# The first k load: from ScalarE's DMA queue to SyncE's, between q and v

## The chip, the cores and the metric

The kernel runs on one core of a Trainium2 chip. The metric is the device time of one launch in microseconds (us). The time before is the median of 3 runs; the profile is of one further execution of the same program.

## The reference

Inputs are q, k and v of shape [8, 8, 576, 64] (batch, heads, positions, head width) and the weights of a mixture of experts, all fp32. What is computed, cut to what matters:

```python
scores = q @ k^T / 8
# heads 0..3: 0 <= i - j < 32
# heads 4..7: 0 <= i - j < 128 and (i - j) % 4 == 0
attn = softmax(where(mask, scores, -1e9))
x = (attn @ v) laid out as [8 * 576, 512]         # 4608 rows, heads side by side

logits = x @ phi                                  # phi [512, 32]: 8 experts, 4 slots each
d = softmax of logits over the 4608 rows          # dispatch
slot_input = d^T @ x                              # [32, 512]
slot_out = relu(slot_input @ w1[e]) @ w2[e]       # w1 [8, 512, 1024], w2 [8, 1024, 512]
out = (softmax of logits over the 32 slots) @ slot_out
```

## The kernel before

**Units and batches.** A unit is a pair of heads of one batch: 4 units to a batch, 32 in all, two pairs of plain windows and two of dilated ones. A loop over u (line 665) runs the stages of neighbouring units one behind the other: scores of the next unit, `values` of this one, the exponentials and masks, the transposes of q and k three units ahead, and the transposes of x of the unit before. Per batch there are also the logits, row weights and slot sums of the batch before, and the selection of v's rows for the next batch. The experts come after the last batch, then the output rows in nine tiles of 512.

**Loads.** Nearly everything is loaded by GpSimd (POOL), whose DMAs turn fp32 into fp16 on the way. For each batch `load_batch` (L179) issues six to seven loads into a buffer, the batch's home. There are eight homes of 16 KB per partition. When a batch is done with, its home takes expert weights (`load_w1`, `load_w2` and others, L266 to L311); a weight load thus waits until the batch that had its home is finished with. The order of POOL's instructions is that of the program (`manual_schedule`, L639).

**The first loads.** Three transfers don't go through POOL, since they are to come before all others: q and k of the first two heads of batch 0 (288 KB each) and v of the first four heads (512 KB). They are loaded as fp32 into `stage`, which takes home 7's place until batch 7 needs it. DVE then casts q and k (L209, one instruction each) while it sets the two heads side by side, PE transposes them (L342), ACT copies the transposes out of PSUM (L343), and the first scores follow. v is cast on ACT (`cast_first_v`, L231), and `select_v` (L238) picks its rows. In the kernel before, q's load is issued by SyncE (SP) and k's by ScalarE (ACT), both on line 74, and v's by SP after q's on line 78. SP issues nothing else until the output (L846, L852).

**Order of the rest.** Two stretches, the head (L644 to L664) and the tail (L702 to L865), have their order on PE, DVE and ACT written out by hand. Before, between and outside them a planner orders the instructions of each engine by its own reckoning. Before the head DVE fills constants (L84 to L126), makes the identity that the transposes need (L148, L149), and does the two casts.

The parts of the kernel that the change touches, with the line numbers of the profile:

Of the kernel before, what the change touches and what calls it, by code (L numbers as in the profile page):

```python
# [46 lines left out]
def kernel(  # L47
# [10 lines left out]
    nc = tc.nc  # L58
# [10 lines left out]
    fixed = keep.tile([128, 128 + QW + 64], FP16, name="fixed")  # L69
    ident, mask = fixed[:, 0:128], fixed[:, 128:]  # L70
    first = {}
    for n, (nm, ten, by) in enumerate((("qp", q, nc.sync), ("kp", k, nc.scalar))):
        first[nm] = stage[0:NP, 768 * n : 768 * n + 768].rearrange("p (g x) -> p g x", g=2)
        by.dma_start(
            out=first[nm],
            in_=ten[0, 0:2].rearrange("h s d -> (h s) d").rearrange("(g p r) d -> p g (r d)", g=2, r=RP),
        )
# [821 lines left out]
```

## Time and profile before

| | |
|---|---|
| median of 3 runs | 180.26 us (180.25 to 180.77) |
| the profiled execution | 180.76 us |
| its span, first to last instruction | 178.5 us |
| mean granted TensorE clock | 0.925 |
| busy: PE, DVE, ACT, POOL | 141.9, 127.6, 117.2, 46.6 us |
| DMA | 41.28 MB in 28,726 packets; HBM read 61.93 MB, written 9.44 MB |

The span counts from the first instruction of any engine to the last; the 2.26 us between it and the execution's time lie around it. Times in the trace are microseconds from the span's start. A line of the timeline gives the start, the duration, the engine (ACTq, SPq and POOL's DMA_DIRECT2D lines are issues of DMAs, not the transfers), the line of the kernel, the operation, output and input, and in brackets how long the engine had been idle and what it waited for. A line of the waits gives who waited for whom: total us, how often, the longest. The DMA queues are named by number: q0 is POOL's, q1 SP's and q10 ACT's. A queue's row gives packets, MB, and the time that its packets took as a share of what 16 engines have.

### The profile page before, as it was taken

The numbers are of one execution on the slowest core, as the hardware profiler recorded it, in microseconds if no ns is written. First come the engines' busy times: TensorE is split into PE (matmuls) and PEld (weight loads), VectorE is DVE, ScalarE is ACT, GpSimd is POOL, SyncE is SP. The second block draws the span as 40 slices with busy tenths as digits, with TensorE's granted clock in tenths as the row PEclk, the third lists the DMA queues.
The fourth block names the chain that finished last, engine by engine and source line by source line (L and its number), as shares of the span: only waits on it lengthen the run. The fifth ranks groups of instructions, "written<-read, shape, count | busy, mean of one in ns | idle before, by whom it ended". The sixth has DMA issues, their size and how long they took to land.

```text
span 178.5 us, 5128 instructions
## 1 busy us (share of the span) xinstructions
PE 141.9 (80%) x2137; PEld 96.7 (54%) x2137; DVE 127.6 (72%) x360; ACT 117.2 (66%) x217; POOL 46.6 (26%) x74
## 2 busy tenths in 40 slices
PE   6697889889999898989989989999689963897000
PEld 2365666575776676667577667666484421542000
DVE  7968998979889789789798988858821110699300
ACT  2568579878897897897988889777321300699100
POOL 7766444444443544000020050042111100000000
PEclk9988699999999999999999999999996996699855
DMA  5999999999999999999999999999999999999996
GB/s 157 240 199 203 201 199 204 200 205 203 203 200 205 201 204 201 224 218 209 224 213 215 224 207 220 220 206 226 215 206 224 208 196 195 242 385 424 431 420 270
DMA packets 28726, 41.28 MB, mean 231 GB/s; under 512 B 1440, under 2 KB 26016, under 8 KB 26144
## 3 DMA queue, kind: packets, MB, share of 16 engines
q0 software_dynamic: 23712, 30.41, 97.1%
q1 hardware_dynamic: 4784, 10.26, 15.0%
q10 hardware_dynamic: 208, 0.29, 0.6%
q8 instruction: 16, 0.26, 0.5%
q14 instruction: 6, 0.05, 0.1%
HBM read 61.93 MB, written 9.44 MB: 400 GB/s over the span
## 4 chain that ended last, share of the span: by engine, by line
PE 38%; DMA 19%; ACT 16%; DVE 14%; issue 4%; POOL 3%; DVEq 0%; ACTq 0%; POOLq 0%
DMA home<-in_moe_w_dram 14%; PE o L486 9%; PE rgx L506 6%; ACT qT L343 5%; PE l L524 5%; DMA home<-in_q_dram 5%; ACT pr L407 4%; PE sel L256 4%; DVE x L491 4%; ACT ot L834 4%; DVE P L433 3%; PE s L381 3%; PE sel L245 3%; PE f L830 3%; PE u L587 2%
## 5 line engine op out<-in xcount | busy, mean ns | idle before, releaser
L491 DVE TENSOR_TENSOR x<-o,rc 128x640 f16<-128x640 f32 x32 | 26.3, 822 | 0.4
L414 ACT ACTIVATE pd<-s 128x640 f16<-128x640 f32 x32 | 21.9, 713 | 2.2 <-PE s L390 2.2
L407 ACT ACTIVATE pr<-s 128x960 f16<-128x960 f32 (+1 forms) x32 | 22.8, 764 | 0.0
L836 DVE TENSOR_SCALAR ot<-f,rrow 128x256 f32<-128x256 f32 (+1 forms) x24 | 13.0, 612 | 6.9 <-PE f L830 6.9
L486 PE MATMUL o<-vd,P 128*128 128x65 f16 x256 | 14.6, 198 | 3.6 <-DVE x L491 3.0
L486 PEld LDWEIGHTS <-P 128*128 128x128 f16 x288 | 12.3, 100 | 7.5 <-DVE x L491 4.1
L512 ACT COPY xT<-rgx 128x512 f16<-128x512 f16 x16 | 9.4, 589 | 10.6 <-PE rgx L506 10.6
L423 DVE TENSOR_TENSOR Pp<-pr,fixed 128x1280 f16<-128x1280 f16 (+1 forms) x32 | 15.6, 501 | 0.1
L486 PE MATMUL o<-vp,Pp 128*128 128x65 f16 x288 | 15.4, 197 | 0.0
L506 PE MATMUL rgx<-fixed,x 128*128 128x128 f16 x155 | 14.0, 222 | 1.7 <-ACT qT L358 0.8
L272 POOL DMA_DIRECT2D home<-in_moe_w_dram x5 | 3.2, 635 | 45.6 <-PE rgq L353 44.1
L343 ACT COPY qT<-rgq 128x576 f16<-128x576 f16 x16 | 10.2, 639 | 6.8 <-PE rgq L342 6.1
L215 POOL DMA_DIRECT2D home<-in_q_dram x15 | 10.0, 668 | 16.2 <-DMA home<-in_v_dram 11.8
L433 DVE TENSOR_TENSOR P<-pd,fixed 128x1024 f16<-128x1024 f16 x16 | 10.9, 679 | 4.7 <-ACT pd L414 4.7
L189 POOL DMA_DIRECT2D home<-in_v_dram x17 | 11.9, 702 | 8.5 <-DMA home<-in_k_dram 4.0
L486 PEld LDWEIGHTS <-Pp 128*128 128x128 f16 x288 | 11.9, 100 | 3.8 <-issue 2.1
L506 PEld LDWEIGHTS <-x 128*128 128x128 f16 x160 | 10.2, 98 | 6.7 <-issue 4.4
L834 ACT ACTIVATE ot<-f,rrow 128x256 f32<-128x256 f32 (+1 forms) x24 | 12.2, 600 | 2.2 <-PE f L830 1.4
L358 DVE COPY kTd<-rgk 128x576 f16<-128x576 f16 x16 | 12.4, 775 | 1.3 <-PE rgk L353 1.3
L830 PE MATMUL f<-so,ET 128*128 128x256 f16 (+1 forms) x48 | 11.4, 361 | 2.2 <-ACT ot L834 1.0
L343 ACT COPY kTp<-rgk 128x576 f16<-128x576 f16 x16 | 10.3, 644 | 2.0 <-PE rgk L342 2.0
L358 ACT COPY qT<-rgq 128x576 f16<-128x576 f16 x16 | 10.3, 641 | 2.0 <-PE rgq L353 1.4
(133 smaller groups left out, 319.0 us busy)
## 6 DMA issues: line engine op xcount, KB each, us to landing
home<-in_moe_w_dram POOLq DMA_DIRECT2D x5, 2048.0 KB, 35.5
home<-in_q_dram POOLq DMA_DIRECT2D x15, 288.0 KB, 10.2
home<-in_k_dram POOLq DMA_DIRECT2D x15, 288.0 KB, 11.0
home<-in_moe_w_dram POOLq DMA_DIRECT2D x4, 1024.0 KB, 28.0
out_dram<-ot SPq DMA_DIRECT2D x4, 1024.0 KB, 9.4
home<-in_v_dram POOLq DMA_DIRECT2D x6, 512.0 KB, 12.7
out_dram<-ot SPq DMA_DIRECT2D x4, 512.0 KB, 3.8
out_dram<-ot SPq DMA_DIRECT2D x1, 2048.0 KB, 7.7
```

The source lines that it names most:

```text
L343: nc.scalar.copy(out=dst[:, 0:S].rearrange("c (p r) -> c p r", r=RP), in_=rg.rearrange("c r p -> c p r"),)
L358: (nc.scalar.copy if nm == "q" else nc.vector.tensor_copy)(out=dst[:, 0:S].rearrange("c (g p a) -> c g p a", g=4, a=3), in_=rg.rearrange(" ...
L407: nc.scalar.activation(out=(pr[:, :, 0 : 3 * QW], pr[:, :, 3 * QW :])[part], in_=st[:, :, 0 : (480, 224)[part]], func=AF.Exp, scale=SCALE,)
L414: nc.scalar.activation(out=pr[:, part].rearrange("p c e t -> p e c t"), in_=st[:, :, 0 : 2 * DW].rearrange("p e (c t) -> p e c t", c=2), f ...
L423: nc.vector.tensor_tensor(out=Pp[:, :, b0 : b0 + nb, 0:w], in0=pr[:, :, b0 * QW : b0 * QW + nb * w].rearrange("p h (t c) -> p h t c", c=w) ...
L433: nc.vector.tensor_tensor(out=P1.rearrange("p a c t -> p (a c) t"), in0=pr[:, :, :, 0:128].rearrange("p a c t -> p (a c) t"), in1=mask[:, ...
L486: nc.tensor.matmul(ot[:, h, blk], lhs, rhs, start=(n == 0), stop=(n == len(mms) - 1), skip_group_check=True)
L491: nc.vector.tensor_tensor(out=xs[b][:, :, 2 * D * hp : 2 * D * hp + 2 * D].rearrange("p t (h d) -> p h t d", h=2), in0=ot[:, :, :, 0:D], i ...
L506: nc.tensor.transpose(rg[:, 128 * blk : 128 * blk + 128], x[:, blk, hl : hl + 128], ident)
L830: nc.tensor.matmul(fp, ET[:, c0 : c0 + 127 * nj + 1 : nj], so[:, d0:d1], start=True, stop=True)
L834: nc.scalar.activation(out=ot[:, j], in_=fp, func=AF.Copy, scale=scale)
L836: nc.vector.tensor_scalar(out=ot[:, j], in0=fp, scalar1=scale, scalar2=None, op0=ALU.mult)
```

## The change

k's load of the first two heads is issued by SyncE in place of ScalarE. In the program it stands after q's load and before v's, all three on SyncE's queue. ScalarE then issues no DMA in the whole kernel. The bytes, the shapes, the destinations and all other instructions in the program are the same.

```diff
@@ -69,9 +69,9 @@
     fixed = keep.tile([128, 128 + QW + 64], FP16, name="fixed")
     ident, mask = fixed[:, 0:128], fixed[:, 128:]
     first = {}
-    for n, (nm, ten, by) in enumerate((("qp", q, nc.sync), ("kp", k, nc.scalar))):
+    for n, (nm, ten) in enumerate((("qp", q), ("kp", k))):
         first[nm] = stage[0:NP, 768 * n : 768 * n + 768].rearrange("p (g x) -> p g x", g=2)
-        by.dma_start(
+        nc.sync.dma_start(
             out=first[nm],
             in_=ten[0, 0:2].rearrange("h s d -> (h s) d").rearrange("(g p r) d -> p g (r d)", g=2, r=RP),
         )
```

## The prediction

> **What bounds the kernel now.** I read the page's slices first, then the chain that ended last, the waits, POOL's timeline, the end, and last the start, where the change is.
>
> The slices of the page:
>
> ```profile
> PE   6697889889999898989989989999689963897000
> ...
> DMA  5999999999999999999999999999999999999996
> GB/s 157 240 199 203 201 199 204 200 205 203 203 200 205 201 204 201 224 218 209 224 213 215 224 207 220 220 206 226 215 206 224 208 196 195 242 385 424 431 420 270
> ```
>
> One slice is 4.46 us. The 16 DMA engines are full from the second slice to the last; only the first has room, half of it. Some 200 to 220 GB/s written is full: POOL's loads turn fp32 into fp16, so twice that is read (the page: 400 GB/s read and written over the span).
>
> The chain in order of time, and PE's waits:
>
> ```profile
> 125.28 25.41 DMA home<-in_moe_w_dram
> 150.73 0.41 PE sop L793 x2
> ```
> ```profile
> PE sop L793 <- DMA home<-in_moe_w_dram: 3.8, 3, 1.7
> ```
>
> The end hangs on the last expert weights. In the timeline PE waits for them 1.15 us at 146.70, 0.90 at 148.00 and 1.71 at 149.99: the work of PE, ACT and DVE could come 3.76 us later before the end noticed. POOL's issues, the other thing that could starve the transfers:
>
> ```profile
> 118.45 0.53 POOL L272 DMA_DIRECT2D home<-in_moe_w_dram  x1 [12.31 <-PE rgq L353]
> ```
>
> This is the last load that waits for compute to free a home. At that moment 4.2 MB are still to be issued (1 + 1 + 0.5 + 0.25 + 0.25 + 1 MB from L697 to L700, in units of 1,048,576 bytes), while the queue view gives q0 6.27 MB in 120:150 and 0.59 MB in 150:165, so with the 1.5 us before them 7.2 MB are still to be moved: 3 MB, or 14 us at 211 GB/s, lie queued ahead. So from about 6 us on the engines run through a fixed amount of work without a gap, and **the end moves only by what the first 6 us gain or lose on the DMA engines**, unless compute slips by 3.76 us.
>
> The start, from the timeline of 0:14:
>
> ```profile
> 0.73 0.43 ACTq L74 DMA_DIRECT2D stage<-in_k_dram  x1
> 0.74 0.38 SPq L74 DMA_DIRECT2D stage<-in_q_dram  x1
> ...
> 1.17 0.44 SPq L78 DMA_DIRECT2D stage<-in_v_dram  x1
> 1.19 1.28 ACT L343 ACT_TABLE_LOAD   x1 [1.19 <-PEq L883]
> ...
> 4.96 0.67 DVE L209 CAST req<-stage 96x768 f16<-96x768 f32 x1
> ...
> 5.71 0.55 DVE L209 CAST rek<-stage 96x768 f16<-96x768 f32 x1
> ...
> 6.32 0.64 ACT L343 COPY qT<-rgq 128x576 f16<-128x576 f16 x1 [3.85 <-PE rgq L342]
> ```
>
> With the times to landing (4.2, 4.5 and 5.5 us) q lands at 4.94, k at 5.23, v at 6.67. DVE is busy up to 4.92, casts q, makes the identity at 5.56, and takes k at 5.71: k has 0.48 us to spare. v is cast on ACT at 7.39 (L231): 0.72 to spare.
>
> The queues in small windows, first 2.2:2.4, then 3.4:3.8, then 5:6 (packets, MB, share of 16 engines):
>
> ```profile
> q10 hardware_dynamic: 5, 0.01, 35.8%
> q1 hardware_dynamic: 9, 0.01, 25.6%
> ```
> ```profile
> q10 hardware_dynamic: 61, 0.09, 60.4%
> q1 hardware_dynamic: 48, 0.06, 42.9%
> ```
> ```profile
> q1 hardware_dynamic: 277, 0.27, 77.8%
> q0 software_dynamic: 79, 0.06, 38.9%
> ```
>
> q10 is ScalarE's queue (k), q1 SyncE's (q, v), q0 POOL's. The first packet of q1 comes at about 1.75, of q10 just after 2.0, of q0 only at 5.3. Up to 3.0 too few packets come; from 3.0 to 3.8 both queues share full engines at 385 GB/s.
>
> **The change part by part.**
>
> *ScalarE.* Its issue (0.43 us) goes. The table load behind it can start up to 0.43 earlier, but ACT then idles 3.85 us until its first copy: nothing.
>
> *SyncE.* It gains one issue of the shape of its q issue (0.38; ACT's row says 0.43), so k is issued at about 1.17 instead of 0.73 and v at 1.55 to 1.60 instead of 1.17. Nothing else waits on SP until the output at 152.79. Even if each landed as long after its issue as now, k would land at 5.67 and v at 7.10, before the 5.71 and 7.39 at which they are taken: no cost.
>
> *The order of the packets.* More likely k lands earlier, because v no longer shares the engines with it. Summed over small windows, q1 and q10 together have moved 209 packets by 3.3 and 422 by 4.0. In the new order the first 208 are q and the next 208 k. With the present 0.6 us from k's last packets (about 4.6) to its landing, q lands near 3.9 and k near 4.6. DVE is at its fills until 4.92, so the casts start when they do now. Gain 0 to 0.04 us on the compute side, which has 3.76 us to spare anyway.
>
> *DMA time, the only term that reaches the end.* The loads are 0.82 + 0.29 = 1.11 MB; at 385 GB/s that is 2.9 us. They take from 1.77 to 6.1, 4.3 us, in which q0 gets 0.08 MB (0.4 us at its own 200 GB/s). So 1.0 us of engine time is lost before 6.1. By the shares of the windows from 2.0 to 3.0 (0.85, 0.61, 0.39, 0.90, 0.78) 0.29 us of it is idle engines; the rest is packets that take long. What one queue in place of two does to this the trace does not show whole; from both sides:
> - against: if q1 alone brings no more than it does now until 3.0, the 39 packets that q10 has by then (0.06 MB) are missing, 0.15 us. If the rate that q1 alone shows at 4.2 to 4.9 (about 250 GB/s) held for all 1.11 MB behind a ramp of 0.5 us, they would end at 6.7 instead of 6.1: 0.55 us as the far end.
> - for: if q's and k's packets come out of one shared source of descriptors (q10's first packet is 0.3 us behind q1's although both were issued at 0.73), the start is no slower, and less mixed; recovering the idle time gives 0.29 us, and all that is lost 1.0 us.
> I take 0. The nearest rows say that full engines don't care how many queues feed them: two queues 385 GB/s at 3.0 to 3.8, q1 alone 358 to 399 GB/s at 5.0 to 5.3, with smaller packets.
>
> The Trainium skill (DMA: Bandwidth & Descriptors, "Issuing engines are not separate DMA queues") says that DMAs issued by several engines run on the same 16 DMA engines, and that issuing from several only saves the sequencer's time. This speaks against the change: two issues side by side become one behind the other. The trace agrees as to the shares (together about 105% with one queue or two). By the rule alone, the 0.43 us of issue would be the whole price and the sum 180.7, which still lies in the forecast's band.
>
> *Sum.* The profiled execution took 180.76 us, 178.5 of span and 2.26 around it. 0 (ACT) + 0 (SP) + 0 (head) + 0 (-0.3 to +0.15) leaves it there. It is at the upper end of the runs (180.25 to 180.77, median 180.26), so for a median I say **180.3**. About 0.3% (0.54 us) is what a measurement of this kernel can tell from no change.
>
> **Rivals.**
> 1. *The planner's order changes (slower).* On PE, DVE and ACT the loop over units is not in written order: the timeline shows L87 and L105 interleaved. If the later issue of k moves something in the planner's reckoning, the loop may come out otherwise. The chain passes L524 at 34.76, 49.32, 63.87 and so on: 14.56 us for a batch. It decides only from 3.76 us over 8 batches, 0.47 us each; at 0.6 us it gives 8 x 0.6 - 3.76 = +1.0, 181.3. Against it: a delay at the start that is not repeated is swallowed, even k issued behind v. Chance 0.20.
> 2. *One queue feeds the engines worse (slower).* The 0.55 us above, 180.8 to 181.0. Against it: q1 alone near 400 GB/s at 5.2, and q0 fills the engines from 5.3 on. Chance 0.10.
> 3. *The start packs better (faster).* Over half of the 1.0 us lost comes back, because q's packets arrive without k's between them and the loads are over when q0 starts: -0.6, 179.7. 169 packets of q1 still come after 5.3, 0.17 MB or 0.43 us at 400 GB/s; a gain beyond that needs q0 to start earlier, for which no row speaks. Something saved in the 2.26 us around the span would come here too. Chance 0.22.
> The forecast, that nothing reaches the end, has 0.48.
>
> **How the numbers follow.** Forecast 179.8 to 180.8; the range reaches to rival 3's gain and to nearly all of rival 1: 179.5 to 181.2. Faster is rival 3 (0.22), the same the forecast (0.48), slower rivals 1 and 2 (0.30).
>
> **What would show it.** After: no q10; two issues of L74 on SPq and then L78; k landing before 5.2 and v by 7.1; casts at 4.96 and 5.71 as now; q0's first packet near 5.3; the loads over by 6.0 to 6.3; PE still waiting for weights near 146.7 and 150. The forecast is wrong if the last waits on DMA move by over 0.5 us, or are gone because compute came late (rival 1), or if q1's last load packet is past 6.6 (rival 2) or before 5.5 (rival 3).

## The result, and the profile after

The kernel after takes 181.84 us (median; 181.22 to 182.51) against 180.48 us for the kernel before in the same rounds (180.25 to 180.77): a ratio of 1.0076, 95% interval 1.0059 to 1.0093. It is slower by 1.4 us. The forecast of 180.3 and its range up to 181.2 are both missed. The profiled execution of after took 182.51 us with a span of 180.5, at the upper end of its runs, as the one of before was at the upper end of its own; between these two the difference is 1.75 us, 2.0 in the span.

The slices of the page (after):

```profile
DMA  5999999999999999999999999999999999899996
GB/s 149 195 202 201 203 199 207 197 206 201 205 199 205 200 205 202 219 220 216 218 214 214 222 209 220 218 216 212 214 220 214 208 198 178 214 385 424 419 436 263
```

The engines are still full from the second slice on (slice 35 alone reads 8). But that slice (4.5 to 9.0 us) moved 195 GB/s where before moved 240; later, slices 34 and 35 show 178 and 214 (before 195 and 242). Everything between looks nearly the same.

The timeline of the start (after; SP's, POOL's, DVE's and ACT's lines picked):

```profile
0.73 0.38 SPq L74 DMA_DIRECT2D stage<-in_q_dram  x1
1.18 0.43 SPq L74 DMA_DIRECT2D stage<-in_k_dram  x1
1.30 0.77 POOL L213 DMA_DIRECT2D home<-in_q_dram  x1 [0.86 <-POOLq L883]
1.65 0.45 SPq L78 DMA_DIRECT2D stage<-in_v_dram  x1
4.85 0.54 DVE L209 CAST req<-stage 96x768 f16<-96x768 f32 x1
5.48 0.64 DVE L209 CAST rek<-stage 96x768 f16<-96x768 f32 x1
10.31 1.04 ACT L231 CAST home<-stage 128x1024 f16<-128x1024 f32 x1 [2.68 <-DMA stage<-in_v_dram]
```

The issues of these loads, with KB and us from issue to landing:

```profile
stage<-in_v_dram SPq DMA_DIRECT2D x1, 512.0 KB, 8.6
stage<-in_q_dram SPq DMA_DIRECT2D x1, 288.0 KB, 3.1
stage<-in_k_dram SPq DMA_DIRECT2D x1, 288.0 KB, 3.7
```

q lands at 3.83 (before 4.94), k at 4.88 (5.23): both earlier, and the casts follow. v lands at 10.25 instead of 6.67. It was issued 0.48 us later and came 3.6 us later. The queues tell when this happened. Before, q0 (POOL) had no packet in 4:4.5. In the windows 3.5:4 and 4:6 of after, each queue with packets, MB and the share of 16 engines:

```profile
q1 hardware_dynamic: 84, 0.11, 86.8%
q0 software_dynamic: 16, 0.01, 18.6%
```
```profile
DMA packets 390, 0.35 MB, mean 174 GB/s; under 512 B 17, under 2 KB 390, under 8 KB 390
q0 software_dynamic: 145, 0.10, 47.4%
q1 hardware_dynamic: 245, 0.24, 40.7%
```

and the window 4:6 of before:

```profile
DMA packets 615, 0.59 MB, mean 296 GB/s; under 512 B 28, under 2 KB 615, under 8 KB 615
q1 hardware_dynamic: 506, 0.50, 86.4%
q0 software_dynamic: 79, 0.06, 19.5%
```

POOL's first packet comes at 3.75 instead of 5.35, with its issue at 1.30 unmoved. From there v and POOL's loads are on the engines together, and the engines move 0.35 MB in two microseconds where they had moved 0.59. (These MB are written bytes, of which POOL's are fp16. Counted as read, where POOL's are twice that, it is 0.44 against 0.65.) The packets of all queues take 88% of the engines' time in that window, against 112% before: so the engines don't only share their time, some of it holds no packet at all. v trickles in until 10; POOL, in spite of its earlier start, is behind by then. Queue q0 in 0:10, after and then before:

```profile
q0 software_dynamic: 755, 0.65, 45.8%
```
```profile
q0 software_dynamic: 916, 0.88, 53.2%
```

0.23 MB less is 1.1 us at the 211 GB/s that full engines write here (12.68 MB of q0 from 60 to 120 us of before). Nothing gives it back: up to 60 us q0 has moved 10.65 MB against 10.87 before, up to 120 us 23.34 against 23.55, up to 145 us 28.63 against 28.85. The chain that ended last still ends as before (after):

```profile
127.25 25.41 DMA home<-in_moe_w_dram
152.71 0.41 PE sop L793 x2
```

The span's 2.0 us are the 1.98 by which this last piece came later (150.73 before). In the queues of 155:156 and 156:157 of after, q0 still has packets; before, its last fell in 154:155.

```profile
q0 software_dynamic: 101, 0.05, 36.0%
```
```profile
q0 software_dynamic: 8, 0.00, 2.8%
```

So POOL's last packet ends at 156.3 instead of 154.4. Of these 1.9 us the lag of 0.23 MB explains 1.1. The rest, some 0.8 us, is a longer tail: in 154:155 q0's packets have 75% of the engines' time and move 0.10 MB, half of what full engines write in a microsecond. That the engines are unevenly behind, and some finish late, would explain it; the views don't list single engines, so this is not shown.

### The profile page after: what moved, and what is told of

Its sections match the earlier page's. It is cut to its first block, busy times and chain, and to the rows that moved or that the text cites. A ratio compares the mean times of both kernels' runs of the same rounds, so it can differ in the third digit from the quotient of the medians.

```text
span 180.5 us, 5128 instructions
## 1 busy us (share of the span) xinstructions
PE 144.8 (80%) x2137; PEld 98.2 (54%) x2137; DVE 127.9 (71%) x360; ACT 117.8 (65%) x217; POOL 47.8 (26%) x74
## 4 chain that ended last, share of the span: by engine, by line
PE 41%; DMA 19%; DVE 17%; ACT 13%; issue 3%; SPq 0%; DVEq 0%; ACTq 0%
DMA home<-in_moe_w_dram 14%; PE o L486 8%; PE rgx L506 5%; DMA stage<-in_v_dram 5%; ACT qT L343 5%; PE sel L256 5%; PE l L524 5%; ACT pr L407 4%; DVE x L491 4%; PE f L830 4%; PE sel L245 4%; DVE ot L836 3%; DVE P L433 3%; PE s L381 3%; PE u L587 2%
## 5 line engine op out<-in xcount | busy, mean ns | idle before, releaser
L407 ACT ACTIVATE pr<-s 128x960 f16<-128x960 f32 (+1 forms) x32 | 22.8, 765 | 0.0
L272 POOL DMA_DIRECT2D home<-in_moe_w_dram x5 | 3.2, 636 | 47.2 <-PE rgq L353 45.8
L189 POOL DMA_DIRECT2D home<-in_v_dram x17 | 13.2, 776 | 8.2 <-DMA home<-in_k_dram 4.6
L343 ACT COPY qT<-rgq 128x576 f16<-128x576 f16 x16 | 10.3, 641 | 7.6 <-PE rgq L342 6.9
L834 ACT ACTIVATE ot<-f,rrow 128x256 f32<-128x256 f32 (+1 forms) x24 | 12.8, 582 | 2.8 <-PE f L830 1.9
L830 PE MATMUL f<-so,ET 128*128 128x256 f16 (+1 forms) x48 | 12.6, 424 | 2.2 <-ACT ot L834 1.2
L245 PE MATMUL sel<-home,pick 32*128 32x256 f16 x128 | 10.5, 289 | 4.1 <-ACT pr L407 4.1
L215 POOL DMA_DIRECT2D home<-in_k_dram x15 | 10.1, 670 | 6.3 <-DMA home<-in_k_dram 3.8
```

The costliest lines, as they stand in the source:

```text
L215: nc.gpsimd.dma_start(out=parts[nm], in_=src)
L245: nc.tensor.matmul(sel[:, n, 0], pick[rows, r].rearrange("p i j -> p (i j)"), raw[rows, :, r, :], start=(r == 0), stop=(r == 3), tile_posi ...
L343: nc.scalar.copy(out=dst[:, 0:S].rearrange("c (p r) -> c p r", r=RP), in_=rg.rearrange("c r p -> c p r"),)
L407: nc.scalar.activation(out=(pr[:, :, 0 : 3 * QW], pr[:, :, 3 * QW :])[part], in_=st[:, :, 0 : (480, 224)[part]], func=AF.Exp, scale=SCALE,)
L830: nc.tensor.matmul(fp, ET[:, c0 : c0 + 127 * nj + 1 : nj], so[:, d0:d1], start=True, stop=True)
```

## The experiments

Two things differ after the start that could each carry the 1.4 us: POOL's lag on the engines, and ACT's wait for v. ACT stands 2.68 us at L231, ahead of the exponentials (L407, 11.26 instead of 8.33), and the last weight load that compute releases (`load_w1(7)`, L272) is issued at 122.20 instead of 118.45. The theory is that v's 512 KB and POOL's loads share the engines badly, because v reaches the engines after POOL's first packet. The rivals:

- O: ACT's wait for v and what follows on compute reach the end.
- P: POOL starts as soon as q and k are through, whatever v does.
- Q: the third of three transfers on one queue is slow by itself (serial issue, or one queue).

Later came two more. R2: POOL's first loads come slowly whenever they start early. And, as a mechanism of the theory, G: an engine doesn't turn to POOL's packets before it is through with its share of the transfer it holds.

The profile of after already speaks against O. Compute is 3.75 us late at `load_w1(7)`, yet PE still waits for the last weights, 1.9 us where it waited 3.8 before:

```profile
PE sop L793 <- DMA home<-in_moe_w_dram: 1.9, 2, 1.7
```

And the late release leaves no gap in the loads: from 120 to 145 us q0 moves 5.29 MB, against 5.30 before.

Each ratio is against runs of the kernel before in the same rounds (medians 180.3 to 180.5). The columns on v and q0 come from the one profiled execution of each kernel, which may lie above or below the median.

| kernel | median us | ratio to before, 95% | v landed | POOL's first packet | q0 MB by 10 us | last q0 packet |
|---|---|---|---|---|---|---|
| before | 180.48 | | 6.67 | 5.35 | 0.88 | 154.4 |
| after | 181.84 | 1.0076 (1.0059 to 1.0093) | 10.25 | 3.75 | 0.65 | 156.3 |
| e1_exp_first | 186.63 | 1.0354 (1.0316 to 1.0392) | 11.25 | 3.6 | 0.67 | 155.8 |
| e2_pool_later | 181.88 | 1.0094 (1.0069 to 1.0120) | 6.75 | 5.4 | 0.70 | 155.5 |
| e3_v_on_act | 180.43 | 1.0007 (0.9994 to 1.0019) | 5.9 | 4.98 | 0.91 | 154.4 |
| e4_q_v_k | 180.41 | 1.0001 (0.9987 to 1.0015) | 5.5 | 4.39 | 0.91 | 154.4 |
| e5_pool_3 | 180.83 | 1.0027 (1.0015 to 1.0039) | 7.75 | 5.17 | 0.81 | 154.8 |
| e6_before_pool_3 | 180.36 | 1.0003 (0.9994 to 1.0011) | 6.5 | 5.5 | 0.88 | 154.4 |
| e7_v_by_pool | 181.73 | 1.0070 (1.0051 to 1.0090) | (POOL) | 3.65 | 1.04, v's 0.26 in it | 155.6 |
| e8_before_v_in_4 | 181.22 | 1.0044 (1.0030 to 1.0058) | 8.8 | 4.19 | 0.83 | 154.9 |
| e9_v_in_4 | 181.61 | 1.0077 (1.0056 to 1.0099) | 9.3 | 3.68 | 0.80 | 155.1 |

Each diff is shortened, and against after, except for e6 and e8, which are against before.

**The wait out of ACT's way (e1).** The cast of v is put behind the first exponentials.

```diff
@@ head, after transposes(0)
-    cast_first_v()
...
-    pr = softmax_parts(0, st)
+    pr = softmax_parts(0, st); cast_first_v()
```

> The changed kernel with ACT's cast of v (L231) behind the two exponentials of unit 0 instead of ahead of them. Theory S (shared engines): POOL's loads enter the DMA engines at 3.7 us instead of 5.3, share them with v, and 0.22 MB of POOL's work (1.1 us) is lost for good; the 2.9 us by which compute is late are mostly swallowed at the end. Then the exponentials come near 8.4 instead of 11.3, compute is some 1 to 3 us earlier, but the last weights land as late as in the changed kernel: 181.4 to 181.9 us. Theory O (order on ACT): the end is late because ACT stood still for v. Then the time goes back to the kernel before: 180.3 to 180.7.

Measured 186.63 us. This edit moved more than it was meant to: the planner put a copy of v's (L234) earlier on DVE, and DVE then stood for a POOL load of v (DVE's waits, total, times, longest):

```profile
DVE vd L234 <- DMA home<-in_v_dram: 13.1, 1, 13.1
```

Compute came some 11 us late (a load of w1 issued at 100.24 instead of 89.22 before), and 6.3 us of it reached the end. The run doesn't decide on O. It shows the size of the cover on compute: nearly 5 us of the 11 were swallowed, somewhat more than the 3.76 us that the waits of before had promised.

**POOL's first load later (e2).** Six memsets of 0.46 us go ahead of POOL's first load; the loop's own are left out, so that POOL's work as a whole is the same.

```diff
@@ L639
+    [nc.gpsimd.memset(hTp[i % 4], 0.0) for i in range(6)]
@@ L695
-            nc.gpsimd.memset(hTp[u - 26], 0.0)
```

> The changed kernel with six memsets (0.46 us each) on POOL ahead of its first load, so that its first packets come at about 5.3 to 6 us instead of 3.7; the four memsets of hTp in the loop are left out for it. Theory S: q, k and v have the engines to themselves, v lands before 7.5, ACT doesn't wait for it, POOL's work by 10 us is again near 0.88 MB: 180.2 to 180.7. Rival Q (one queue is slow by itself: v third in one queue is late whatever POOL does): v lands after 8.5, and POOL's own delay comes on top: 182 or more.

Measured 181.88 us, as slow as after, and outside what the theory had forecast. v is third in one queue here and lands 5.1 us after its issue, so Q is false. ACT has no wait for v at all. What was lost here was POOL's own time. Its first issue came at 3.42, each next one 0.5 to 0.8 us later, and the engines ran short of work. The window 7.5:9 of e2, and then of before:

```profile
q0 software_dynamic: 143, 0.16, 99.5%
```
```profile
q0 software_dynamic: 251, 0.32, 120.3%
```

In its last microsecond (8:9) q0's packets took 69% of the engines' time and moved 0.11 MB, against 116% and 0.21 before. q0 had moved 0.70 MB by 10 us. The delay was too long, so the run put one cause of the same lag in place of another, and decides neither on the sharing nor on O.

**v on ScalarE's queue (e3).** q and k stay on SP's.

```diff
@@ L78
-    nc.sync.dma_start(out=first_v, in_=v[0, 0:4, ...
+    nc.scalar.dma_start(out=first_v, in_=v[0, 0:4, ...
```

> q and k on SyncE's queue as in the changed kernel, v on ScalarE's. Theory S with its cause (two busy queues of SyncE and ScalarE keep POOL's first packets out, one does not): POOL's first packet near 4.6 to 5.3, v landed by about 7, 180.3 to 180.8. Rival P (POOL's packets begin when q and k are through, whatever the queues): first packet at 3.7 to 4, v lands after 8, 181.4 to 182.

Measured 180.43 us: before's time. v is issued at 0.73 and is on the engines before POOL's first packet, which comes at 4.98. Here k is the late one (it lands at 6.7, and DVE waits 0.96 us for it), and that costs nothing.

**One queue, in the order q, v, k (e4).** Nothing goes on ScalarE's queue.

```diff
@@ L73, in the loop over q (n = 0) and k (n = 1), ahead of the load of each
+        n and nc.sync.dma_start(out=first_v, in_=v[0, 0:4, 0:512, :] ...)
@@ L78
-    nc.sync.dma_start(out=first_v, in_=v[0, 0:4, ...
```

> All three on SyncE's queue in the order q, v, k. Theory S: POOL's first packet comes at about 3.7 again, v lands near 6, k shares the engines with POOL and lands at 7 to 9 instead of 4.9; POOL is as far behind as in the changed kernel (0.65 to 0.7 MB by 10 us), so the last weights are as late: 181.3 to 182. Theory O (only what ACT waits for counts): compute is late by the late k, 2 to 3 us, so also 181 to 182; rival Q: with v second it lands by 6 and only k is late, POOL not behind, 180.5 to 181.

Measured 180.41 us: before's time, with an interval of 0.13% below to 0.15% above no change. It has all that the diff did (no load on ScalarE, three loads on one queue, three issues in a row), except for the place of v. Here it is k that comes late (timeline, DVE; the issues' line for v; q0 in 0:10):

```profile
7.56 0.56 DVE L209 CAST rek<-stage 96x768 f16<-96x768 f32 x1 [1.84 <-DMA stage<-in_k_dram]
```
```profile
stage<-in_v_dram SPq DMA_DIRECT2D x1, 512.0 KB, 4.3
```
```profile
q0 software_dynamic: 942, 0.91, 55.4%
```

DVE waits 1.84 us for k and compute runs some 2.5 us late (`load_w1(7)` at 120.97, 118.45 before), and the end stays where it was (a span of 178.6 us, 178.5 before). So a compute delay of this size is swallowed, and POOL's first packet as early as 4.39 costs nothing when v is ahead of it. P is false: POOL's first packet comes while k is still on its way (it lands at 7.5). Nor do two busy queues have to keep POOL out, the cause named ahead of e3: here there is one, and nothing is lost. The theory in its first form, by which any of the three loads beside POOL's would cost this, had forecast 181.3 to 182, and that is false too: k's 288 KB and POOL's packets were on the engines together without a loss (in 5:6 all packets take 118% of the engines' time, where in after they take 77%).

**A small delay of POOL (e5), and its control (e6).** Three memsets ahead of POOL's first load, in after and in before.

```diff
@@ L639, the loop's memsets stay
+    [nc.gpsimd.memset(hTp[i % 4], 0.0) for i in range(3)]
```

> The changed kernel with three memsets (0.46 us each) on POOL ahead of its first load, nothing else. POOL issues its first load at about 2.0 us instead of 1.30, so that its packets are ready near 4.4 instead of 3.7. Theory F (whoever comes first: v must be on the engines before POOL's first packet): v has begun by then, POOL's first packet comes at 5 to 5.4, v lands before 7.3, POOL has moved 0.80 to 0.90 MB by 10 us, 180.3 to 180.9. Rival R (any sharing of the engines between v and POOL costs this): first packet at 4.4, v lands after 9, 0.65 to 0.70 MB by 10 us, 181.5 to 182.

> The kernel before with the same three memsets on POOL ahead of its first load: the control of the run with the changed kernel. Theory F: POOL's packets waited for v until 5.3 anyway, so nothing moves: 0.85 to 0.90 MB by 10 us, 180.2 to 180.7. If POOL's lead in issuing is what matters (the run with six memsets had gaps on the engines from 7.75 to 9.0), it loses up to the 0.7 us here: 0.75 to 0.80 MB, 180.7 to 181.1.

Measured 180.83 us for e5 and 180.36 for e6, both as the theory had it. In after, giving POOL more work and a later start (first load issued at 2.04 instead of 1.30) makes the kernel some 0.9 us faster (ratios 1.0027 and 1.0076, each to before in its own rounds); in before, where v holds the engines until 5.35 anyway, it does nothing. Lines of e5: POOL's timeline, the issue of v, and the window 5:5.5.

```profile
2.04 0.77 POOL L213 DMA_DIRECT2D home<-in_q_dram  x1
```
```profile
stage<-in_v_dram SPq DMA_DIRECT2D x1, 512.0 KB, 6.1
```
```profile
q1 hardware_dynamic: 132, 0.13, 81.7%
q0 software_dynamic: 8, 0.01, 10.4%
```

v, still third in SP's queue, lands 6.1 us after its issue instead of 8.6. This is the experiment that e2 was to be: the order of arrival decides, and 0.74 us of delay takes back some 0.9 of the 1.4 us.

**v by POOL itself (e7).** v of the first heads is POOL's first load, as fp16, without the cast.

```diff
@@ L78
-    nc.sync.dma_start(out=first_v, ...
@@ load_batch, first line
+        b == 0 and load_v("vp", 0, 4, 0, t[:, 6144:7168])
@@ L650
-    cast_first_v()
```

> q and k on SyncE's queue as in the changed kernel, v of the first heads loaded by POOL as its first load, as fp16 and into its place (ACT's cast L231 is not needed and left out). Theory F: no third burst stands against POOL's packets; they begin at 3.6 to 3.8, v lands by 6.5, POOL has moved its 0.9 MB and v's 0.26 MB (1.15 to 1.2 MB in all) by 10 us, 179.8 to 180.5. Rival R2 (POOL's first loads come slowly whenever they start early): 0.95 MB or less in all, 181.3 to 182.

Measured 181.73 us, where the theory had 179.8 to 180.5 and R2 181.3 to 182 (with 0.95 MB of q0 or less by 10 us; it was 1.04). POOL's other loads stand at 0.78 MB by 10 us, 0.10 behind before's, or 0.5 us; yet the time is up by 0.70%, 1.3 us, and the last packet 1.2 us late. The lag has a price of its own: in 4:6 the engines are full (106%) and q0 moves 0.26 MB, as much as v has. Loaded by POOL, v thus takes some 2 us of full engines, where from SP's queue its 0.52 MB would take about 1.4 us (an estimate, by the 379 GB/s of before in 5:5.3). So this run is no clean test of the theory. It doesn't exclude R2; what stands against R2 is e4, where POOL's first packet comes at 4.39 instead of 5.35 and POOL isn't behind by 10 us (0.91 MB). And the lag at 10 us alone doesn't give the time; the tail is longer here too.

**v in four transfers (e8 in before, e9 in after).** One head each, all on SP's queue, in place of one transfer. Evenly spread, each engine has 32 records of v to bring as one transfer (512 of 1 KB over 16 engines), and 8 at a time as four.

```diff
@@ L78
-    nc.sync.dma_start(out=first_v, in_=v[0, 0:4, 0:512, :] ...
+    [nc.sync.dma_start(out=first_v[:, h : h + 1], in_=v[0, h : h + 1, 0:512, :] ...) for h in range(4)]
```

> The kernel before (k on ScalarE's queue) with v loaded by four transfers of one head each on SyncE's queue instead of one of four heads. Theory G (an engine doesn't turn from SyncE's or ScalarE's transfer to POOL's until its share of that transfer is through, and v as one transfer thereby keeps POOL out until 5.3): POOL's first packet comes at 3.7 to 4.3, v's last quarter lands at 8 or later, POOL has moved 0.65 to 0.80 MB by 10 us, 180.9 to 182. Rival H (POOL's first packet has nothing to do with how v is cut; it waits for the number of queues or for the bytes ahead of it): first packet near 5.3, 0.85 to 0.90 MB, 180.2 to 180.7.

> The changed kernel with v loaded by four transfers of one head each. Theory G: POOL's first packet again at 3.6 to 3.8, as in the changed kernel; v's quarters take turns with POOL's shares, the last lands at 8 to 11; 0.60 to 0.75 MB by 10 us, 181.3 to 182.2. Rival H: nothing is different from the changed kernel, 181.5 to 182 with v landing at 10.2.

Measured 181.22 us for e8: before is made slower by 0.44% (0.30 to 0.58) by nothing but cutting v. The window 4:4.5 of e8:

```profile
q1 hardware_dynamic: 90, 0.08, 69.7%
q10 hardware_dynamic: 31, 0.03, 26.9%
q0 software_dynamic: 17, 0.01, 16.7%
```

POOL's first packet is there at 4.19 instead of 5.35. ACT's cast of v comes at 8.86 after a wait of 0.38 us. It is 1.47 us later than before (7.39), less than the delay that e4 shows to be covered:

```profile
8.86 1.04 ACT L231 CAST home<-stage 128x1024 f16<-128x1024 f32 x1 [0.38 <-DMA stage<-in_v_dram]
```

So 0.8 us (0.44% of 180.3) are lost with k on ScalarE's queue, q and v on SP's, and a compute delay that is covered. That is the theory's effect in the kernel of before, and it came as G had it. G isn't the only reading: the cut also spreads v's issues, so that the last quarter is issued at 2.61 instead of 1.17, and no run separates the two. e9 gave 181.61 us and a first packet at 3.68, much as after: v comes behind POOL's first packet there in any case. By 10 us both are less behind than G had it (0.83 and 0.80 MB, which is 0.2 and 0.4 us), and this lag is the smaller part of what they lose (0.8 and 1.4 us).

The last column of the table goes with the time in all runs but e1 (where compute sets the end): 154.4 with 180.4, 154.8 with 180.8, 154.9 with 181.2, 155.1 with 181.6, 155.5 to 155.6 with 181.7 to 181.9. In e8 and e9 it explains only part: their spans grew by 0.9 and 1.1 us, the last packet came 0.5 and 0.8 later. In after the profile (156.3, at 182.51) is above the median, in e2 (181.42) below it. What is shown for after is that its loss hangs on the place of v relative to POOL's first packet (e4 and e5 take all or most of it back, each without changing what is loaded; e6 is the control), and reaches the end as the last POOL load. Left open is why engines that carry both are used so badly from 4 to 6 us in after (174 GB/s), why k in e4 doesn't do the same, and why the tail grows by more than the mean lag. On this last point the runs give a hint: taking from the delay of the last packet what the lag at 150 us is worth, 0.9 us are left in after, 0.7 in e7 and 0.4 in e8 and e9, where POOL's first packet comes before 4.2, and 0.1 to 0.2 in e2 and e5, where it comes after 5.

None of the versions is faster than before. e3, e4 and e6 equal it.

## Why the prediction was wrong

**Right steps.** What bounds the kernel held: the end moved by what the engines lost at the start, and the 3.76 us of slack covered compute. Only the first 6 us were too short for it, as the loss ran on to 10, and the tail came on top. ACT's late v made compute 2.9 us late at the start and 3.75 by `load_w1(7)`, and PE still waits 1.71 us for weights at its last expert (timeline, after):

```profile
152.01 0.51 PE L793 MATMUL sop<-home,hTp 128*32 128x256 f16 x6 [1.71 <-DMA home<-in_moe_w_dram]
```

ACT's saved issue and SP's added one cost nothing. q near 3.9 (3.83) came as said; k, said near 4.6, landed at 4.88. The sum behind it had 422 packets by 4.0 where the trace has 405, and the 0.17 MB that q1 still has after 5.3 are 0.16; neither moves the forecast. By the rule of the Trainium skill on issuing engines (DMA: Bandwidth & Descriptors, "Issuing engines are not separate DMA queues") the price was to be the 0.43 us of the serial issue; e4 has that serial issue and is level with before, so the price was zero. The rule's other half, that the loads run on the same 16 engines whichever engine issues them, agrees with it.

**The step that failed: the DMA time, taken as 0 with −0.3 to +0.15 around it.** It measured +1.1 us of lag by 10 us, with the longer tail on top, and 1.4 us in the time. Two sentences carried it. "Full engines don't care how many queues feed them" holds for SP's and ACT's queues, and better than I had it: q1 alone brought 352 GB/s in 2.5:3.5, where two queues had brought 300. The window 2.5:3.5 of after, and of before:

```profile
q1 hardware_dynamic: 245, 0.35, 104.6%
```
```profile
q1 hardware_dynamic: 104, 0.16, 48.4%
q10 hardware_dynamic: 92, 0.14, 43.3%
```

It didn't hold for POOL's queue beside v's transfer. The other sentence was "q0's first packet near 5.3", carried over from before as if 5.3 were POOL's own latency. It was v's doing: v was issued early enough to be on the engines when POOL's packets became ready at about 3.7 (3.65 to 3.75 in after, e7 and e9), and they had to wait until it was nearly through; delaying POOL in before by 0.74 us (e6) changed nothing. The trace of before had the hint, four microseconds from POOL's issue (1.30) to its first packet (5.35), against one for SP's, and I didn't ask what it waited for.

**v's landing.** "Even if each landed as long after its issue as now, v would land at 7.10" assumed the same company on the engines; 10.25 was measured. ACT's cover of 0.72 us was gone and ACT waited 2.68 us, which the slack took.

**Rivals.** The first (the planner's order) didn't come: the order on PE and POOL is the same instruction by instruction, on ACT but for the load's issue, and on DVE but for two memsets of 0.07 us (L655). The second had the right sign, with the wrong mechanism (one queue fed worse) and too small a price (at most 0.55 us). The third had its premise fulfilled, since the start does pack better and q0 does start earlier, and that was just what cost the time. No rival had a queue that starts earlier as a loss.

## What to carry to other kernels

Ask not only which queue is free, but which transfer will hold the DMA engines when another queue's first packet becomes ready: here a bulk load that was one place further back fell behind POOL's first packet and cost 1.4 us, while the same three loads on the same queue in another order cost nothing. A late first packet in a trace may be the effect of another transfer and not the queue's own latency, so an edit that delays that transfer moves it. In a kernel that is bound by DMA from start to end, as this one, what the first ten microseconds lose is still there at the end, while compute delays within the slack aren't.

## What the runs showed of the hardware

- POOL's first packet came at 3.75 us or at 5.35 with the same issue at 1.30, by whether v's transfer was on the engines yet. Cut into four, with its last quarter issued at 2.61 instead of 1.17, v kept it out only until 4.19 (e8). The Trainium skill (DMA: Bandwidth & Descriptors, "Queues, rings and completion order") says that an engine goes round its queues and finishes a packet of several descriptors before it turns to the next queue; the change from one transfer to four agrees in kind, though no run here counts descriptors to a packet (the rows counted as packets here hold 1 KB each for v).
- With v and POOL's loads together the engines moved 174 GB/s in 4:6, their packets taking 88% of the engines' time, against 296 GB/s and 112% before, when POOL's were kept out until 5.35. In e4, where v was ahead and k was the load that came beside POOL's, it was 301 GB/s and 118%.
- Cutting a transfer into four, with the same bytes from the same queue, cost 0.44%; delaying POOL by 0.74 us made after some 0.9 us faster, and left before as it was (0.9994 to 1.0011).
